# The low-rank mixer on array tiles: A summed in column tiles, V.A in row tiles, u kept by feature chunk

## The chip, the cores and the metric

One NeuronCore of a Trainium2 chip runs the program. Its engines each follow their own instruction list and wait for one another through semaphores: PE (TensorE, matrix products; its weight loads are listed as PEld), DVE (VectorE), ACT (ScalarE), POOL (GpSimd) and SP (SyncE, which here only issues DMAs). PE reads SBUF and writes PSUM, which has eight banks of 512 float32 values per partition; DVE and ACT take the products out of PSUM. The metric is the device time of one execution in microseconds. The kernel before took 309.22 us, the median of three runs (308.85 to 309.67).

## The reference

For 8 batches of 8 heads, 576 tokens and 64 features a head, a cosine-weighted linear attention gives x; a mixer over tokens of rank 32 and a two-layer network over features follow:

```
phi(t)  = [relu(t) cos(theta_s), relu(t) sin(theta_s)]       theta_s = pi/2 * s/576
kv      = phi(k)^T v,  z = sum_s phi(k)                        per batch and head
x       = phi(q) kv / (phi(q) z + 1e-6)                        [576, 512] per batch, heads side by side
A^T     = x^T U          [512, 32]                             U: [576, 32]
u       = x + (A^T V)^T                                        V: [32, 576]
out     = u + relu(u w_ch1) w_ch2                              w_ch1: [512, 2048], w_ch2: [2048, 512]
```

All inputs and the output are float32; the kernel multiplies in bfloat16 and sums in float32.

## The kernel before

The 576 tokens of a batch are four chunks of 128 (index c) and a tail of 64; the tails of two batches, an even and an odd one, share the 128 partitions of one tile, and the network runs over four such pairs of batches. The 512 features are four chunks of 128 (index d), the 2048 hidden features sixteen (index j).

The order of all work is written out by hand. The network gives `slots`: for each pair 16 turns `g1_main` of the even batch (u^T times w_ch1, four matmuls of 512 tokens' columns, then a relu on ACT), 16 of the odd one, four `g1_tail`, and 36 turns `g2_part` (hid times w_ch2, four matmuls of 512 columns; after every fourth, DVE adds u and the output tile is stored). In pair 0, sixteen turns of `g2_part` come between the two batches. A turn is about 0.86 us on PE. Everything else is hung on turns through `todo` and is issued behind that turn: the attention of the batches that come later, from `attention_plan(b)` for batches 2 to 7 (the start turn `w` from `PLAN`, offsets within it), and by hand for batch 1 (`at(...)`). Batch 0 has no network to hide behind and runs first, in `first_chain`. Engines take their instructions in the order in which they are issued here.

For one batch the steps around the change are:

- `x_unit`, `x_two`: PE multiplies phi(q) with kv for one token chunk into PSUM, DVE normalises into `x_bf` (tokens on partitions, [128, 4 chunks, 512 features]) or the tail's `x_tl`.
- `A_unit` (L416): U^T x. The rank is 32, so each token chunk c takes one of the four column tiles of the array (32 columns, `tile_position=(0, c * R)`) and leaves its own partial sum over its 128 tokens in partitions 32c to 32c+31 of one bank; the tail adds a quarter of the features into each. The cast into `A_sb` (128 x 512, bfloat16) keeps four partial sums.
- `u_unit` (L434; `u_two`, L969, for batch 1): V^T A for one token chunk is one matmul of 128 rows and 512 columns. `V_bf` holds V four times over, one copy in each 32 partitions, so that this matmul also adds the four partial sums. DVE then adds x (L448, L982) and leaves u for this token chunk in `u_bf`. The tail's matmuls (L444) do the same for two batches at once.
- `utr_dma` (L461): SP issues two DMA transposes, one for token chunks 0 and 1, one for 2 and 3, that bring u^T into `uT` for `g1_main`; a third for the tail.

Batch 0 does without the DMA: `open_mm` (L780) transposes x on PE into PSUM, `uTd_mm` (L502) adds A^T V to it there, and a cast takes the sum into `uT`; `u_dma` (L475) later transposes it back into `u_bf` for the output. Its A is made in two halves of 256 features (`a_mm`, L765 and L773).

PSUM is shared by tags: "g" (three banks) and "o" (two) belong to the network's two layers, "T" is one bank, "X" two. `spare(turn)` gives the one of "g" and "o" that the network is not using in that turn. The inputs' staging tiles `qst`, `kst`, `vst` exist once each; the loads of a later batch go out on SP when the casts have read them.

Ahead of all, `keep_warm` multiplies zeros on PE until q has come.

Of the kernel before, what the change touches and what calls it, by code (L numbers as in the profile page):

```python
# [17 lines left out]
def kernel(  # L18
# [163 lines left out]
    A_sb = [const.tile([P, DM], BF16, name=f"A_sb{i}") for i in range(4)]  # L182
# [7 lines left out]
    def keep_warm(n, tag, bufs, w=512):  # L190
        w_ps = ps.tile([P, 512], FP32, tag=tag, bufs=bufs, name="w_ps")
        for _ in range(n):
            nc.tensor.matmul(  # L193
                out=w_ps[:, 0:w], lhsT=zero[:, 0:P], rhs=zero[:, 0:w], start=True, stop=True
            )
# [220 lines left out]
    def A_unit(b, tag, bufs, eng=None, n0=0, n1=DM, a_ps=None):  # L416
        if a_ps is None:
            a_ps = ps.tile([P, DM], FP32, tag=tag, bufs=bufs, name="a_ps")
        w = (n1 - n0) // 4
        for c in range(4):  # L420
            nc.tensor.matmul(  # L421
                out=a_ps[c * R : c * R + R, n0:n1], lhsT=U_bf[:, c, :],
                rhs=x_of(b, c)[:, n0:n1], start=True, stop=False, tile_position=(0, c * R),
            )
        for c in range(4):
            ns = slice(n0 + c * w, n0 + c * w + w)
            nc.tensor.matmul(
                out=a_ps[c * R : c * R + R, ns], lhsT=U_bf[:, 4 + b % 2, :],
                rhs=x_of(b, 4)[:, ns], start=False, stop=True, tile_position=(0, c * R),
            )  # L430
        cast(eng or V_, A_of(b)[:, n0:n1], a_ps[:, n0:n1])
        return a_ps

    def u_unit(b, c, tag, bufs):  # L434
        if b not in u_bf:
            u_bf[b] = pool.tile([P, 4, DM], BF16, tag="u_bf", bufs=3, name="u_bf")
        if c == 4:
            u_tl[b // 2] = pool.tile([P, DM], BF16, tag="u_tl", bufs=2, name="u_tl")
        va = ps.tile([P, DM], FP32, tag=tag, bufs=bufs, name="va_ps")
        if c < 4:  # L440
            nc.tensor.matmul(out=va, lhsT=V_bf[:, c, :], rhs=A_of(b), start=True, stop=True)  # L441
        else:
            for i in range(2):
                nc.tensor.matmul(  # L444
                    out=va[tail(i), :], lhsT=V_tl, rhs=A_of(b - 1 + i), start=True, stop=True,
                    tile_position=(0, i * TS),
                )
        nc.vector.tensor_tensor(  # L448
            out=u_bf[b][:, c, :] if c < 4 else u_tl[b // 2], in0=x_of(b, c), in1=va,
            op=ALU.add,  # L450
        )
# [9 lines left out]
    def utr_dma(b, c0, c1):  # L461
        if c0 < 4:
            uT_alloc(b)
            nc.sync.dma_start_transpose(
                out=uT[b][:, c0:c1, :, :].rearrange("m c d t -> m (c d) t"),
                in_=u_bf[b][:, c0:c1, :].rearrange("p c n -> p (c n)"),
            )
        else:
            uTt_alloc(b // 2)
            nc.sync.dma_start_transpose(out=uT_tl[b // 2], in_=u_tl[b // 2])  # L470

    def u_dma(b, c0, c1):
        if b not in u_bf:
            u_bf[b] = pool.tile([P, 4, DM], BF16, tag="u_bf", bufs=3, name="u_bf")
        nc.sync.dma_start_transpose(  # L475
            out=u_bf[b][:, c0:c1, :].rearrange("t c (d n) -> t (c d) n", n=P),
            in_=uT[b][:, c0:c1, :, :].rearrange("n c d t -> n (c d t)"),
        )
# [18 lines left out]
    def uTd_evac(b, d, eng):  # L497
        cast(eng, uT[b][:, :, d, :], uT_ps[b, d])

    def uTd_mm(b, d):  # L500
        t = uT_ps[b, d]
        nc.tensor.matmul(  # L502
            out=t.rearrange("m c t -> m (c t)"), lhsT=A_of(b)[:, d * P : d * P + P],
            rhs=V_bf.rearrange("r c t -> r (c t)"), start=False, stop=True,
        )

    def uTt_direct(pr, tag, bufs, eng):
        uTt_alloc(pr)
        t = ps.tile([P, 4, P], FP32, tag=tag, bufs=bufs, name="uTt_ps")
        for d in range(4):  # L510
            dd = slice(d * P, d * P + P)
            nc.tensor.matmul(
                out=t[:, d, :], lhsT=x_tl[:, dd], rhs=ident, start=(d == 0), stop=False
            )
            for i in range(2):
                nc.tensor.matmul(
                    out=t[:, d, tail(i)], lhsT=A_of(2 * pr + i)[:, dd], rhs=V_tl,
                    start=False, stop=(d == 3 and i == 1),
                )
        cast(eng, uT_tl[pr], t)  # L520

# [5 lines left out]
    def g1_main(b, j, half=False):  # L527
        if b not in hid:
            hid[b] = pool.tile([P, NJ, 512], BF16, tag="hid", bufs=2, name="hid")
        g_ps = g_open.pop((b, j), None)  # L530
        d0 = 0 if g_ps is None else 2
        if g_ps is None:
            g_ps = ps.tile([P, 512], FP32, tag="g", bufs=3, name="g_ps")
        if half:
            g_open[b, j] = g_ps
        for d in range(d0, 2 if half else 4):
            nc.tensor.matmul(  # L537
                out=g_ps.rearrange("p (c t) -> p c t", c=4),
                lhsT=w1_bf[:, d, j * P : j * P + P],
                rhs=uT[b][:, :, d, :],  # L540
                start=(d == 0),
                stop=(d == 3),
            )
        if half:
            return
        nc.scalar.activation(  # L546
            out=hid[b][:, j, :], in_=g_ps, func=AF.Relu, bias=0.0, scale=1.0
        )

    def g_half(b, d, js):  # L550
        for j in js:
            if d == 0:
                g_open[b, j] = ps.tile([P, 512], FP32, tag="g", bufs=3, name="g_ps")
            nc.tensor.matmul(  # L554
                out=g_open[b, j].rearrange("p (c t) -> p c t", c=4),
                lhsT=w1_bf[:, d, j * P : j * P + P],
                rhs=uT[b][:, :, d, :],
                start=(d == 0),
                stop=False,
            )  # L560
# [23 lines left out]
    def g2_part(pr, cc, part):  # L584
# [6 lines left out]
        if cc == 4:  # L591
            b, lhs, c, u = None, hid_tl[pr], 0, u_tl[pr]
        else:
            b, c = (2 * pr, cc) if cc < 4 else (2 * pr + 1, cc - 5)
            lhs, u = hid[b], u_bf[b][:, c, :]
# [14 lines left out]
        if js[-1] < NJ - 1:  # L610
# [3 lines left out]
            out=o_sb[:, cols], in0=u[:, cols], in1=o[:, cols], op=ALU.add  # L614
# [54 lines left out]
    def attention_plan(b):  # L669
# [39 lines left out]
        for c in range(4 + odd):  # L709
            put(a_at + 2 + c, u_unit, c, tag=True)  # L710
        put(a_at + 4, utr_dma, 0, 2)
        put(a_at + 6, utr_dma, 2, 4)
        if odd:
            put(a_at + 8, utr_dma, 4, 5)
# [45 lines left out]

    def a_mm(b, a_ps, n0, n1, cs):
        w = (n1 - n0) // 4
        for c in cs:
            if c < 4:
                nc.tensor.matmul(  # L765
                    out=a_ps[c * R : c * R + R, n0:n1], lhsT=U_bf[:, c, :],
                    rhs=x_of(b, c)[:, n0:n1], start=True, stop=False,
                    tile_position=(0, c * R),
                )
                continue  # L770
            for i in range(4):
                ns = slice(n0 + i * w, n0 + i * w + w)
                nc.tensor.matmul(  # L773
                    out=a_ps[i * R : i * R + R, ns], lhsT=U_bf[:, 4 + b % 2, :],
                    rhs=x_of(b, 4)[:, ns], start=False, stop=True, tile_position=(0, i * R),
                )
# [8 lines left out]
    def first_chain(b):  # L785
# [42 lines left out]
        a_mm(b, a_ps, 0, 256, range(5))  # L828
        cast(A_, A_of(b)[:, 0:256], a_ps[:, 0:256])
# [9 lines left out]
        a_mm(b, a_ps, 256, 512, range(5))  # L839
        cast(A_, A_of(b)[:, 256:512], a_ps[:, 256:512])  # L840
# [17 lines left out]
    keep_warm(86, "X", 1, P)  # L858
# [110 lines left out]
    def u_two(b, c0):  # L969
        if b not in u_bf:  # L970
            u_bf[b] = pool.tile([P, 4, DM], BF16, tag="u_bf", bufs=3, name="u_bf")
        if c0 == 0:
            t = ps.tile([P, 2, 512], FP32, tag="X", bufs=1, name="va2_ps")
            va = [t[:, 0, :], t[:, 1, :]]
        else:
            va = [ps.tile([P, DM], FP32, tag="T", bufs=1, name="va_ps"), side["g"]]
        for c in (c0, c0 + 1):
            nc.tensor.matmul(
                out=va[c - c0], lhsT=V_bf[:, c, :], rhs=A_of(b), start=True, stop=True
            )  # L980
        for c in (c0, c0 + 1):
            nc.vector.tensor_tensor(  # L982
                out=u_bf[b][:, c, :], in0=x_of(b, c), in1=va[c - c0], op=ALU.add
            )

    at(22, lambda: A_unit(1, "T", 1, A_))
    for n, c0 in enumerate((0, 2)):
        at(23 + n, lambda c0=c0: u_two(1, c0))
        at(23 + n, lambda c0=c0: utr_dma(1, c0, c0 + 2))
    at(32, lambda: u_unit(1, 4, *O2))  # L990
# [71 lines left out]
```

## Time and profile before

| what | us |
|---|---|
| median of the runs | 309.22 |
| the profiled execution | 311.43 |
| its span, first to last instruction | 309.7 |
| PE busy in it | 301.4 |
| DVE busy | 149.7 |
| ACT busy | 140.7 |
| POOL busy | 46.5 |
| four V.A matmuls of a batch (L441), each | 0.379, starts 0.216 apart when back to back |
| the add of u for one chunk (L448), mean | 0.686 |
| the cast of A on DVE (L110, 128 x 512) | 0.692 |

A matmul's length in the trace includes its way through the array, in which the next has already begun; what a matmul costs PE is the distance from start to start. A group of lines in the timeline is written as its first start, the time from that to the last end, and the count. The granted clock is the share of TensorE's full clock that the chip gave it, 0.998 on the mean of this execution.

### The profile page before, as it was taken

Reading aid. Unit: us, or ns where it says so; the run is one execution under the profiler, and the core shown is the slowest. Engines: PE = TensorE matmul, PEld = TensorE weight load, DVE = VectorE, ACT = ScalarE, POOL = GpSimd, SP = SyncE. Lnnn points to the kernel's source line nnn. Section 1 sums busy time; section 2 is a strip of 40 time slices with the busy share of each in tenths; the row PEclk is TensorE's granted clock in tenths of the full one; section 3 lists DMA queues with packets and bytes.
Section 4 is the critical chain, followed back from the end, with each engine's and each line's share of the span. In section 5 each row is a group of like instructions: output and inputs, shape, how many; then the busy total and the mean of one; then the engine's idle time right before and its main releaser. Section 6 shows DMA issues by size and latency. Waiting matters only on the chain.

```text
span 309.7 us, 5867 instructions
## 1 busy us (share of the span) xinstructions
PE 301.4 (97%) x2392; PEld 161.0 (52%) x2392; DVE 149.7 (48%) x353; ACT 140.7 (45%) x241; POOL 46.5 (15%) x86
## 2 busy tenths in 40 slices
PE   8999999999999999999999999999999999999992
PEld 8676454448455444664454444664455444554441
DVE  4978574864867692256247590166336500001211
ACT  2945912365771566589000566589100566620000
POOL 8411200020020015004311400004221000000000
PEclk9999999999999999999999999999999999999999
DMA  7999999899999989798999399812941220002212
GB/s 209 353 260 255 247 183 226 228 220 237 290 156 225 295 186 244 220 296 180 196 276 341 99 167 243 249 19 77 222 110 70 68 51 2 0 22 82 68 68 70
DMA packets 90702, 54.28 MB, mean 175 GB/s; under 512 B 58484, under 2 KB 87444, under 8 KB 90676
## 3 DMA queue, kind: packets, MB, share of 16 engines
q1 hardware_dynamic: 84020, 43.72, 61.2%
q0 software_dynamic: 5984, 9.60, 13.0%
q10 hardware_dynamic: 672, 0.59, 0.7%
q8 instruction: 19, 0.31, 0.4%
q14 instruction: 7, 0.06, 0.1%
HBM read 36.86 MB, written 9.44 MB: 149 GB/s over the span
## 4 chain that ended last, share of the span: by engine, by line
PE 86%; DMA 6%; SPq 3%; DVE 3%; issue 1%; DVEq 0%
PE o_ps L603 38%; PE g_ps L537 31%; DMA vst<-in_v_dram 6%; PE gt_ps L569 5%; PE kv_ps L305 3%; PE x_ps L396 2%; PE va_ps L441 2%; SPq L74 1%; SPq L87 1%; PE a_ps L421 1%; PE t_ps L322 1%; DVE u_bf L982 1%; DVE v_ext L110 1%; DVE k_p L266 0%; PE g_ps L554 0%
## 5 line engine op out<-in xcount | busy, mean ns | idle before, releaser
L546 ACT ACTIVATE hid<-g_ps 128x512 bf16<-128x512 f32 x128 | 76.2, 599 | 106.2 <-PE g_ps L537 106.2
L603 PE MATMUL o_ps<-w_bf,hid 128*128 128x512 bf16 (+2 forms) x528 | 119.7, 372 | 0.0
L537 PE MATMUL g_ps<-uT,w_bf 128*128 128x512 bf16 x506 | 115.4, 379 | 0.0
L537 PEld LDWEIGHTS <-w_bf 128*128 128x128 bf16 x506 | 48.0, 98 | 56.7 <-issue 1.9
L603 PEld LDWEIGHTS <-hid 128*128 128x128 bf16 x528 | 48.5, 98 | 51.9 <-issue 1.1
L613 DVE TENSOR_TENSOR o_sb<-u_bf,o_ps 128x512 f32<-128x512 bf16 (+2 forms) x33 | 22.1, 670 | 57.0 <-PE o_ps L603 56.8
L628 POOL DMA_DIRECT2D out_dram<-o_sb x18 | 11.4, 632 | 122.2 <-DVE o_sb L613 48.1
L110 POOL CAST v_ext<-vst 128x512 bf16<-128x512 f32 (+1 forms) x26 | 18.5, 735 | 48.8 <-DMA vst<-in_v_dram 48.7
L110 DVE CAST kv<-kv_ps 128x260 bf16<-128x260 f32 (+1 forms) x15 | 6.4, 427 | 36.1 <-PE kv_ps L305 36.1
L448 DVE TENSOR_TENSOR u_bf<-x_bf,va_ps 128x512 bf16<-128x512 bf16 x24 | 16.5, 686 | 10.2 <-PE va_ps L441 10.2
L369 DVE TENSOR_SCALAR rec<-x_ps 128x8 f32<-128x8 f32 (+2 forms) x39 | 6.3, 162 | 20.1 <-PE x_ps L396 19.4
L569 PE MATMUL gt_ps<-uT_tl,w_bf 128*128 128x128 bf16 x256 | 15.9, 219 | 0.0
L406 DVE TENSOR_TENSOR x_bf<-x_ps,rec 128x512 bf16<-128x512 f32 x22 | 15.2, 692 | 0.8
L569 PEld LDWEIGHTS <-w_bf 128*128 128x128 bf16 x256 | 14.7, 98 | 0.9
L603 PE MATMUL o_ps<-w_bf,hid_tl 128*128 128x512 bf16 x64 | 14.8, 379 | 0.0
L305 PEld LDWEIGHTS <-k_p 128*128 128x128 bf16 x256 | 11.2, 97 | 3.4 <-issue 0.3
L576 ACT ACTIVATE hid_tl<-gt_ps 128x512 bf16<-128x512 f32 x16 | 9.6, 598 | 6.6 <-PE gt_ps L569 6.6
L305 PE MATMUL kv_ps<-v_ext,k_p 128*128 128x65 bf16 (+1 forms) x256 | 11.9, 193 | 0.2
L264 ACT ACTIVATE k_p<-kst,sinw 128x512 bf16<-128x512 f32 x17 | 12.0, 717 | 0.0
L266 DVE TENSOR_SCALAR q_p<-qst,cosw 128x512 bf16<-128x512 f32 x21 | 9.9, 481 | 3.2 <-DMA qst<-in_q_dram 3.2
L193 PE MATMUL w_ps<-zero 128*128 128x128 bf16 (+1 forms) x97 | 10.1, 269 | 1.2 <-DVE zero L119 1.2
L266 DVE TENSOR_SCALAR k_p<-kst,cosw 128x512 bf16<-128x512 f32 x20 | 10.4, 542 | 1.8 <-DMA kst<-in_k_dram 1.8
(143 smaller groups left out, 252.0 us busy)
## 6 DMA issues: line engine op xcount, KB each, us to landing
kst<-in_k_dram SPq DMA_DIRECT2D x14, 512.0 KB, 8.0
qst<-in_q_dram SPq DMA_DIRECT2D x13, 512.0 KB, 5.3
vst<-in_v_dram SPq DMA_DIRECT2D x12, 512.0 KB, 8.0
out_dram<-o_sb POOLq DMA_DIRECT2D x18, 256.0 KB, 3.8
w_bf<-in_moe_w_ch_dram POOLq DMA_DIRECT2D x8, 512.0 KB, 12.9
out_dram<-o_sb SPq DMA_DIRECT2D x13, 256.0 KB, 2.4
qst<-in_q_dram SPq DMA_DIRECT2D x2, 640.0 KB, 8.0
kst<-in_k_dram SPq DMA_DIRECT2D x2, 640.0 KB
```

Source lines behind the costliest of these rows:

```text
L110: eng.tensor_copy(out=o, in_=i)
L264: nc.scalar.activation(out=o, in_=i, func=AF.Relu, bias=0.0, scale=w)
L266: eng.tensor_scalar(out=o, in0=i, scalar1=0.0, scalar2=w, op0=ALU.max, op1=ALU.mult)
L305: nc.tensor.matmul(out=acc[:, i, :], lhsT=k_of(b, c, h), rhs=v_tl[:, h, 0:n] if c == 4 and b < 2 else vx[:, c, h, 0:n], start=(c == 0), st ...
L406: nc.vector.tensor_tensor(out=x_of(b, c, rows).rearrange("p (g i d) -> p g i d", g=2, d=D), in0=view[:, :, :, 0:D], in1=rec[rows].unsqueez ...
L448: nc.vector.tensor_tensor(out=u_bf[b][:, c, :] if c < 4 else u_tl[b // 2], in0=x_of(b, c), in1=va, op=ALU.add,)
L537: nc.tensor.matmul(out=g_ps.rearrange("p (c t) -> p c t", c=4), lhsT=w1_bf[:, d, j * P : j * P + P], rhs=uT[b][:, :, d, :], start=(d == 0) ...
L546: nc.scalar.activation(out=hid[b][:, j, :], in_=g_ps, func=AF.Relu, bias=0.0, scale=1.0)
L569: nc.tensor.matmul(out=g_ps[:, jj, :], lhsT=w1_bf[:, d, j * P : j * P + P], rhs=uT_tl[pr][:, d, :], start=(d == 0), stop=(d == 3),)
L603: nc.tensor.matmul(out=o[:, cols], lhsT=lhs[:, j, c * P : c * P + P], rhs=w2_bf[:, j, cols], start=(j == 0), stop=(j == NJ - 1),)
L613: nc.vector.tensor_tensor(out=o_sb[:, cols], in0=u[:, cols], in1=o[:, cols], op=ALU.add)
L628: eng.dma_start(out=out[b].rearrange("(m k) n -> m k n", k=9)[:, c : c + 6 : 5, cols], in_=o_sb[:, cols],)
```

## The change

- A: each column tile now belongs to a feature chunk j, not to a token chunk. It takes the five token chunks (the tail first) one after another in the same 128 columns of PSUM, so that the sum over tokens is whole. `A_sb` becomes 128 x 128: partitions 32j to 32j+31 hold the 32 ranks of feature chunk j. The cast is of 128 columns.
- V.A: feature chunk j is now in 32 partitions of its own, so the products for the four j are put on the four row tiles of the array (32 rows each, `tile_position=(j * R, 0)`), each into its own PSUM bank, with `c` as the outer loop: sixteen matmuls of 128 columns instead of four of 512. They take both banks of "X" and two spare ones at the same time (`four_banks`). The tail is eight such matmuls, on 32 x 64 tiles.
- u: the four adds are now by feature chunk, and `u_bf` and `uT` are laid out feature chunk first. The two transposes of a batch are of feature chunks 0 and 1, and 2 and 3, and are issued one turn earlier in the plan. The output's adds read u in four runs of 128.
- Batch 0: the halves of A are column tiles 0, 1 and 2, 3; `uTd_mm` uses one row tile of 32 rows.
- The zero products in front are 4 of 512 columns and 72 of 128, instead of 86 of 128.

```diff
-    A_sb = [const.tile([P, DM], BF16, name=f"A_sb{i}") for i in range(4)]
+    A_sb = [const.tile([P, P], BF16, name=f"A_sb{i}") for i in range(4)]
...
-    def keep_warm(n, tag, bufs, w=512):
+    def keep_warm(n, tag, bufs, short=0):
         w_ps = ps.tile([P, 512], FP32, tag=tag, bufs=bufs, name="w_ps")
-        for _ in range(n):
+        for i in range(n + short):
+            w = 512 if i < n else P
...
+    def A_mm(b, a_ps, js):
+        for c in ORD:
+            for j in js:
+                nc.tensor.matmul(
+                    out=a_ps[j * R : j * R + R, 0:P],
+                    lhsT=U_bf[:, c if c < 4 else 4 + b % 2, :],
+                    rhs=x_of(b, c)[:, j * P : j * P + P], start=(c == ORD[0]), stop=(c == ORD[-1]),
+                    tile_position=(0, j * R),
+                )
+
+    def A_unit(b, tag, bufs, eng=None):
+        a_ps = ps.tile([P, DM], FP32, tag=tag, bufs=bufs, name="a_ps")
+        A_mm(b, a_ps, range(4))
+        cast(eng or V_, A_of(b), a_ps[:, 0:P])
+
+    def four_banks(*spare):
+        t = ps.tile([P, 2, 512], FP32, tag="X", bufs=1, name="va4_ps")
+        more = [
+            x if not isinstance(x, tuple)
+            else ps.tile([P, 512], FP32, tag=x[0], bufs=x[1], name="va_ps")
+            for x in spare
+        ]
+        return [t[:, 0, :], t[:, 1, :]] + more
...
+    def u_mm(b, *spare):
...
+        va[b] = four_banks(*spare)
         for c in range(4):
...
+            for j in range(4):
+                rows = slice(j * R, j * R + R)
                 nc.tensor.matmul(
+                    out=va[b][j][:, c * P : c * P + P], lhsT=V_bf[rows, c, :],
+                    rhs=A_of(b)[rows, :], start=True, stop=True, tile_position=(j * R, 0),
                 )
...
+    def u_add(b, j):
+        ns = slice(j * P, j * P + P)
         nc.vector.tensor_tensor(
+            out=u_bf[b][:, j, :, :], in0=x_bf[b][:, :, ns],
+            in1=va[b][j].rearrange("p (c n) -> p c n", c=4), op=ALU.add,
+        )
+
+    def u_tail(pr, *spare):
+        u_tl[pr] = pool.tile([P, DM], BF16, tag="u_tl", bufs=2, name="u_tl")
+        vt = four_banks(*spare)
+        for i in range(2):
+            for j in range(4):
+                rows = slice(j * R, j * R + R)
+                nc.tensor.matmul(
+                    out=vt[j][tail(i), 0:P], lhsT=V_tl[rows, :],
+                    rhs=A_of(2 * pr + i)[rows, :], start=True, stop=True,
+                    tile_position=(j * R, i * TS),
+                )
+        for j in range(4):
+            ns = slice(j * P, j * P + P)
+            nc.vector.tensor_tensor(
+                out=u_tl[pr][:, ns], in0=x_tl[:, ns], in1=vt[j][:, 0:P], op=ALU.add
+            )
...
     def uTd_mm(b, d):
         t = uT_ps[b, d]
         nc.tensor.matmul(
-            out=t.rearrange("m c t -> m (c t)"), lhsT=A_of(b)[:, d * P : d * P + P],
-            rhs=V_bf.rearrange("r c t -> r (c t)"), start=False, stop=True,
-        )
...
+            out=t.rearrange("m c t -> m (c t)"), lhsT=A_of(b)[d * R : d * R + R, :],
+            rhs=V_bf[d * R : d * R + R].rearrange("r c t -> r (c t)"),
+            start=False, stop=True, tile_position=(d * R, 0),
+        )
...
-        for c in range(4 + odd):
-            put(a_at + 2 + c, u_unit, c, tag=True)
-        put(a_at + 4, utr_dma, 0, 2)
-        put(a_at + 6, utr_dma, 2, 4)
+        plan.append((w + a_at + 2, lambda: u_mm(b, *[spare(w + a_at + 2)] * 2)))
+        for j in range(4):
+            put(a_at + 2 + j, u_add, j)
+        put(a_at + 3, utr_dma, 0, 2)
+        put(a_at + 5, utr_dma, 2, 4)
         if odd:
+            plan.append(
+                (w + a_at + 7, lambda: u_tail(b // 2, *[spare(w + a_at + 7)] * 2))
+            )
             put(a_at + 8, utr_dma, 4, 5)
...
-        a_mm(b, a_ps, 0, 256, range(5))
-        cast(A_, A_of(b)[:, 0:256], a_ps[:, 0:256])
+        A_mm(b, a_ps, (0, 1))
+        cast(A_, A_of(b)[0:TS, :], a_ps[0:TS, 0:P])
...
-    keep_warm(86, "X", 1, P)
+    keep_warm(4, "X", 1, 72)
...
     at(22, lambda: A_unit(1, "T", 1, A_))
-    for n, c0 in enumerate((0, 2)):
-        at(23 + n, lambda c0=c0: u_two(1, c0))
-        at(23 + n, lambda c0=c0: utr_dma(1, c0, c0 + 2))
-    at(32, lambda: u_unit(1, 4, *O2))
+    at(23, lambda: u_mm(1, T1, side["g"]))
+    for j in range(4):
+        at(23, lambda j=j: u_add(1, j))
+    for c0 in (0, 2):
+        at(23, lambda c0=c0: utr_dma(1, c0, c0 + 2))
+    at(32, lambda: u_tail(0, T1, O2))
     at(33, lambda: utr_dma(1, 4, 5))
```

More of the change, by code (lines that the diff above doesn't have):

```diff
@@ L414, in A_of @@
         return A_sb[b % 4]
[L416 to L419, printed above, removed]
-        for c in range(4):
-            nc.tensor.matmul(
-                out=a_ps[c * R : c * R + R, n0:n1], lhsT=U_bf[:, c, :],
-                rhs=x_of(b, c)[:, n0:n1], start=True, stop=False, tile_position=(0, c * R),
-            )
[L425 to L429, printed above, removed]
-            )
-        cast(eng or V_, A_of(b)[:, n0:n1], a_ps[:, n0:n1])
-        return a_ps
@@ L434, in u_unit @@
[L434 to L451, printed above, removed]
+    def A_mm(b, a_ps, js):
[7 more added lines that the diff above has]
+                )
@@ new lines @@
+    va = {}
+    def u_mm(b, *spare):
+        if b not in u_bf:
+            u_bf[b] = pool.tile([P, 4, 4, P], BF16, tag="u_bf", bufs=3, name="u_bf")
+        va[b] = four_banks(*spare)
+        for c in range(4):
+            for j in range(4):
[4 more added lines that the diff above has]
+                )
@@ new lines, in u_add @@
+    def u_add(b, j):
[10 more added lines that the diff above has]
+                rows = slice(j * R, j * R + R)
+                nc.tensor.matmul(
+                    out=vt[j][tail(i), 0:P], lhsT=V_tl[rows, :],
[4 more added lines that the diff above has]
+            ns = slice(j * P, j * P + P)
+            nc.vector.tensor_tensor(
+                out=u_tl[pr][:, ns], in0=x_tl[:, ns], in1=vt[j][:, 0:P], op=ALU.add
+            )
@@ L464, in utr_dma @@
             nc.sync.dma_start_transpose(
-                out=uT[b][:, c0:c1, :, :].rearrange("m c d t -> m (c d) t"),
-                in_=u_bf[b][:, c0:c1, :].rearrange("p c n -> p (c n)"),
+                out=uT[b][:, c0:c1, :, :].rearrange("m d c t -> m (d c) t"),
+                in_=u_bf[b][:, c0:c1, :, :].rearrange("p d c n -> p (d c n)"),
             )
@@ L473, in u_dma @@
         if b not in u_bf:
-            u_bf[b] = pool.tile([P, 4, DM], BF16, tag="u_bf", bufs=3, name="u_bf")
+            u_bf[b] = pool.tile([P, 4, 4, P], BF16, tag="u_bf", bufs=3, name="u_bf")
         nc.sync.dma_start_transpose(
-            out=u_bf[b][:, c0:c1, :].rearrange("t c (d n) -> t (c d) n", n=P),
-            in_=uT[b][:, c0:c1, :, :].rearrange("n c d t -> n (c d t)"),
+            out=u_bf[b][:, c0:c1, :, :].rearrange("t d c n -> t (d c) n"),
+            in_=uT[b][:, c0:c1, :, :].rearrange("n d c t -> n (d c t)"),
         )
@@ L497, in uTd_evac @@
     def uTd_evac(b, d, eng):
-        cast(eng, uT[b][:, :, d, :], uT_ps[b, d])
+        cast(eng, uT[b][:, d, :, :], uT_ps[b, d])
     def uTd_mm(b, d):
@@ L502, in uTd_mm @@
         nc.tensor.matmul(
-            out=t.rearrange("m c t -> m (c t)"), lhsT=A_of(b)[:, d * P : d * P + P],
-            rhs=V_bf.rearrange("r c t -> r (c t)"), start=False, stop=True,
-        )
[L507 to L520, printed above, removed]
+            out=t.rearrange("m c t -> m (c t)"), lhsT=A_of(b)[d * R : d * R + R, :],
+            rhs=V_bf[d * R : d * R + R].rearrange("r c t -> r (c t)"),
+            start=False, stop=True, tile_position=(d * R, 0),
+        )
     hid, hid_tl = {}, {}
@@ L539, in g1_main @@
                 lhsT=w1_bf[:, d, j * P : j * P + P],
-                rhs=uT[b][:, :, d, :],
+                rhs=uT[b][:, d, :, :],
                 start=(d == 0),
@@ L556, in g_half @@
                 lhsT=w1_bf[:, d, j * P : j * P + P],
-                rhs=uT[b][:, :, d, :],
+                rhs=uT[b][:, d, :, :],
                 start=(d == 0),
@@ L591, in g2_part @@
         if cc == 4:
-            b, lhs, c, u = None, hid_tl[pr], 0, u_tl[pr]
+            b, lhs, c = None, hid_tl[pr], 0
+            u = u_tl[pr].rearrange("p (j n) -> p j n", n=P)
         else:
             b, c = (2 * pr, cc) if cc < 4 else (2 * pr + 1, cc - 5)
-            lhs, u = hid[b], u_bf[b][:, c, :]
+            lhs, u = hid[b], u_bf[b][:, :, c, :]
         if last:
@@ L613, in g2_part @@
         nc.vector.tensor_tensor(
-            out=o_sb[:, cols], in0=u[:, cols], in1=o[:, cols], op=ALU.add
+            out=o_sb[:, cols].rearrange("p (j n) -> p j n", n=P),
+            in0=u[:, cols.start // P : cols.stop // P, :],
+            in1=o[:, cols].rearrange("p (j n) -> p j n", n=P), op=ALU.add,
         )
@@ L759, in warm @@
         keep_warm(n, *tag)
[L761 to L776, printed above, removed]
     def open_mm(b, d, t, cs):
@@ L838, in first_chain @@
         uTd_evac(b, 1, V_)
-        a_mm(b, a_ps, 256, 512, range(5))
-        cast(A_, A_of(b)[:, 256:512], a_ps[:, 256:512])
+        A_mm(b, a_ps, (2, 3))
+        cast(A_, A_of(b)[TS:P, :], a_ps[TS:P, 0:P])
         u2 = ps.tile([P, 2, 512], FP32, tag="X", bufs=1, name="u2")
@@ L967 @@
             at((16, 17, 18, 19, 20)[n], lambda c=c: x_unit(1, c, "X", 1))
[L969 to L984, printed above, removed]
-    at(22, lambda: A_unit(1, "T", 1, A_))
-    for n, c0 in enumerate((0, 2)):
-        at(23 + n, lambda c0=c0: u_two(1, c0))
-        at(23 + n, lambda c0=c0: utr_dma(1, c0, c0 + 2))
-    at(32, lambda: u_unit(1, 4, *O2))
+    at(22, lambda: A_unit(1, "T", 1, A_))
+    at(23, lambda: u_mm(1, T1, side["g"]))
[4 more added lines that the diff above has]
+    at(32, lambda: u_tail(0, T1, O2))
     at(33, lambda: utr_dma(1, 4, 5))
```

## The prediction

> **What bounds the kernel now.** I read the page first: busy shares, slices, the chain that ended last.
>
> ```profile
> PE 301.4 (97%) x2392; PEld 161.0 (52%) x2392; DVE 149.7 (48%) x353; ACT 140.7 (45%) x241; POOL 46.5 (15%) x86
> ...
> PE 86%; DMA 6%; SPq 3%; DVE 3%; issue 1%; DVEq 0%
> PE o_ps L603 38%; PE g_ps L537 31%; DMA vst<-in_v_dram 6%; PE gt_ps L569 5%; PE kv_ps L305 3%; PE x_ps L396 2%; PE va_ps L441 2%; SPq L74 1%; SPq L87 1%; PE a_ps L421 1%; PE t_ps L322 1%; DVE u_bf L982 1%; DVE v_ext L110 1%; DVE k_p L266 0%; PE g_ps L554 0%
> ```
>
> PE is busy 97%, at a granted clock of 0.998, and it holds 86% of the chain. So what PE no longer has to stream is time saved, unless a wait takes it. Next, PE's timeline around one batch's A and V.A (columns: start, length, engine, line, tiles, count).
>
> ```profile
> 83.30 0.59 PE L603 MATMUL o_ps<-w_bf,hid 128*128 128x512 bf16 x2
> 83.82 0.40 PE L421 MATMUL a_ps<-x_bf,U_bf 128*32 128x512 bf16 x4
> 84.05 0.23 PE L427 MATMUL a_ps<-x_tl,U_bf 128*32 128x128 bf16 x4
> 84.21 1.90 PE L603 MATMUL o_ps<-w_bf,hid 128*128 128x512 bf16 x8
> 85.95 0.38 PE L441 MATMUL va_ps<-A_sb,V_bf 128*128 128x512 bf16 x1
> ```
>
> Starts count, not lengths. Eight matmuls of 512 columns fill 84.21 to 85.95, 0.216 us each. Four matmuls on the four column tiles of the array (`128*32`) take 0.23 us together: they run side by side, and the next four follow 0.01 us after a single one's 0.216. The two L603 matmuls before them end their turn at 83.30 + 2 x 0.216 = 83.73, and A begins at 83.82: 0.09 us of drain on the way into tiles. On the way out, 84.05 to 84.21 holds 128 columns (0.056 by L569, 16 in 0.89 us), 0.01 of stagger and 0.096 of drain. So A costs 84.21 - 83.73 = 0.48 us. The four V.A matmuls L441 stand alone between L603's; the next of these starts at 86.16, so each costs 0.216: 0.86 us a batch. The tail's V.A is the third cost:
>
> ```profile
> 109.22 0.59 PE L537 MATMUL g_ps<-uT,w_bf 128*128 128x512 bf16 x2
> 109.75 0.41 PE L444 MATMUL va_ps<-A_sb,V_tl 128*64 128x512 bf16 x2
> 110.09 0.82 PE L537 MATMUL g_ps<-uT,w_bf 128*128 128x512 bf16 x3
> ```
>
> From 109.65 to 110.09 it is 0.44 us, two matmuls side by side and two drains. Last, the only wait of PE after 25 us, and the chain into it:
>
> ```profile
> 59.28 9.15 DMA vst<-in_v_dram
> ...
> 70.46 0.34 DVE v_ext L110
> ```
>
> ```profile
> 70.45 0.59 PE L305 MATMUL kv_ps<-v_ext,k_p 128*128 128x65 bf16 x4
> 70.87 0.19 PE L305 MATMUL kv_ps<-v_ext,k_tl 128*128 128x65 bf16 x1
> ```
>
> Four matmuls of 65 columns, 0.03 us each, would be followed at 70.57; the next starts at 70.87. For these 0.30 us PE stands until batch 2's v has been loaded and cast. What PE saves before 70.8 us only lengthens this wait.
>
> **The change part by part.**
>
> *V.A in row tiles.* Removed per batch: four matmuls of 512 columns, 0.863 us. Added: sixteen of 128 columns, 32 rows each, in four rounds (c) over four row tiles (j). No row tiles run side by side in this trace; the bounds are the nearest rows. From below, they behave as the column tiles do: a round is 0.056 + 0.01 = 0.066 us, four are 0.264, and with the drains 0.093 and 0.096 the block is 0.45 us, 0.41 less. From above, they go one after another: 16 x 0.056 + 0.19 = 1.08 us, 0.22 more. The drains I take as those of a 32-row matmul, which the trace has:
>
> ```profile
> 14.08 0.34 PE L876 MATMUL z_ps<-v_tl,k_p 128*128 128x1 bf16 x8
> 14.35 0.41 PE L229 MATMUL v_ps<-V_nat,four 32*128 32x512 bf16 x2
> 14.70 0.35 PE L876 MATMUL z_ps<-v_tl,k_p 128*128 128x1 bf16 x8
> ```
>
> The eight one-column matmuls, 0.025 us each, end their turn at 14.26, and L229 starts at 14.35: 0.09 again; its 512 and 64 columns, 0.216 + 0.027, leave 0.10 until 14.70. I take the lower bound, 0.45, since four streams with four sets of weights at once is what the column tiles show, and each row tile here writes a bank of its own. The Trainium skill's page "TensorE: Matmul & The Clock Gate", section "Measured speedup vs the span model", gives 3.07 times for four row tiles of 32 rows and 512 columns; by it the block is an estimated 0.863 / 3.07 + 0.19 = 0.47 us and the sum below 0.1 us smaller. No run shown here has that case yet.
>
> *A in column tiles.* Removed: four matmuls of 512 and four of 128 columns. Added: five rounds of four matmuls of 128 columns. The columns per tile are the same 640. Five rounds of 0.066 and the drains are 0.52 us against 0.48: +0.04. From above, a round may be held by its four weight loads; the nearest row is the second A of batch 0, where a round of 256 columns follows in 0.12 us (21.63 to 21.75 below). Five of those make 0.79, +0.31. I take +0.04; the 128-column round is the same shape as L427.
>
> *The tail's V.A* becomes eight matmuls of 128 columns on eight tiles (32 by 64): 0.10 + 0.03 of stagger + 0.056 + 0.10 = 0.28 us against 0.44, -0.16; in a row it would be 8 x 0.056 + 0.19 = 0.64, +0.20.
>
> *Batch 0's first chain* (20 to 25 us):
>
> ```profile
> 21.09 0.61 PE L502 MATMUL uT_ps<-V_bf,A_sb 128*128 128x512 bf16 x2
> 21.63 0.31 PE L765 MATMUL a_ps<-x_bf,U_bf 128*32 128x256 bf16 x4
> 21.75 0.22 PE L773 MATMUL a_ps<-x_tl,U_bf 128*32 128x64 bf16 x4
> ```
>
> Each half of A now uses two column tiles: five rounds of 0.059 instead of 0.12 + 0.04, +0.14 twice. The casts shrink from 128x256 (384 ns on ACT) to 64x128: ACT's 598 for 512 columns and 384 for 256 give an estimated 277, -0.11 twice, on the path into L502. L502's pairs sit on two row tiles and two banks: 0.22 instead of 0.43 with two new drains, 0 to -0.2 each; but the evacuation of the first of a pair then starts with the second's, 0.2 later than now. I take +0.1 in all, between -0.2 and +0.4 (row tiles in sequence: 0.2 more). It passes on: batch 1's u, the transposes and the loads that lead to 70.8 all follow it.
>
> *Evacuations.* The A cast on DVE falls from 128x512 (692 ns) to 128x128 (an estimated 265, by the cast kv's 407 for 256 columns); the adds u_bf stay four of 686, with x_bf read in runs of 128 (the normalisation L406 writes in runs of 64 in 692). The tail's add becomes four of 128 columns (o_sb's of that shape takes 0.286): 1.1 for 0.69 us. Hidden: DVE is 48% busy and PE waits for none of it. Uncovered, it would be the banks: V.A now takes X's two and two spare banks at once, and a tail takes all four again five turns of 0.86 us later. Batch 3's fourth add comes behind two q casts on DVE and ends near 109.2, the tail starts near 110.2: 1 us of cover. If it is gone, PE stands for what is missing, three times.
>
> *Transposes.* Same two DMA transposes of eight blocks, issued one turn earlier, on SP; each now needs two adds as before. Behind them on SP are the next loads and the q transposes. For batch 1 the second transpose left at 52.59 behind the add that ended at 52.41; the new V.A's last round starts at 49.28 + 0.09 + 0.21 = 49.58, the first add 0.27 later (as A's cast at 84.33 behind 84.06), and four adds of 0.61 from start to start end at 52.4: unchanged, and with it the loads into 70.8. The transposes land 1 to 3 us ahead of L537's first use (batch 1: 55.68 against 57.1). The u_bf of batch 0, transposed back, now needs both halves for every output: landed at 49.58, first used at 54.66, hidden.
>
> *The zero products first:* 86 of 128 columns end at 7.7 us, and PE then waits for q until 8.41. At the slow clock (0.107 for 128 columns until 4.7 us) four of 512 and 72 of 128 end at 7.8: 0. If they ran past 8.41 every us would count until v's casts at 16.15, which wait for a load anyway.
>
> **The sum.** Behind 70.8 us: six V.A, 6 x -0.41 = -2.46; six A, +0.22; three tails, -0.48; in front of it -0.53 that the wait swallows (0.30 grows to 0.8), and +0.1 of the first chain. Together -2.6 us. The profiled execution took 311.43 us, a span of 309.7 and 1.7 around it, and becomes 308.8; against the median of the runs, 309.22, it is 306.6. The next wait that could bite is batch 3's v: cast until 89.63, used at 90.27, 0.6 us of slack, of which 0.37 goes. Batch 4's casts end at 120.87 for 125.64.
>
> **Rivals.** 0.3% (0.93 us) is about what a measurement of this kernel can tell from no change.
>
> Slower: the row tiles don't overlap. V.A 1.08: 6 x 0.22 = +1.31; A +0.22; tails +0.60; first chain +0.3; before 70.8 0.46, of which the present wait takes 0.30, so +0.16. Together +2.6, 311.8 us. For it: no row of the trace has two row tiles at once. Against: the column tiles. It decides where a V.A block passes 0.89 us (nothing gained) and 1.04 (slower).
>
> Little gained: pairs of load and matmul are issued at 0.025 us as in L876, whatever the tile. V.A is then 16 x 0.025 + 0.056 + 0.19 = 0.65, 6 x -0.22; A +0.04; tails 0; first chain +0.1: -1.0, 308.2 us. Against: L421's four loads and matmuls stand within 0.01 us.
>
> A's rounds wait for their weights: twenty loads where there were eight, and a round at the row's 0.12 us: 6 x 0.31 for 6 x 0.04, 308.2 us. For it: that row is no lower, since 256 columns fill it. Against: its loads are issued with the round before and needed 0.07 us later at the shortest (21.68 to 21.75), about a 128-column round. The Trainium skill's page "TensorEngine Tiling (Array Packing)", "Restrictions", has column tiles lose the fast weight load, and the page "TensorE: Matmul & The Clock Gate", "LDWEIGHTS (loading the stationary operand)", makes 32 columns 27 ns; four in a row would be an estimated 0.107 us a round, and 307.8 us. No run shown here tells.
>
> Hidden anyway: the loads follow PE so closely that the later batches wait as batch 2 does. If only the last two batches kept their gain, it would be 2 x 0.37 + 0.16: 308.4 us. Against: 4.8 us of cover at batch 4.
>
> A wait for banks at V.A or at a tail, up to 1 us at each of three odd batches: 306.6 + 3 = 309.6.
>
> **How the numbers follow.** Forecast 0.68, in itself 305.9 to 307.6 (A's rounds up to 0.09, the first chain's ends); row tiles in sequence 0.12; issue 0.04; weights 0.06; loads 0.05; banks 0.05. Faster (below 308.3): the forecast and half of issue, weights and loads, 0.75. Same: their other half and most of banks, 0.12. Slower (above 310.1): 0.13. The range reaches from 305.7 to 309.3: it leaves out the sequence and some banks.
>
> **What would show it.** V.A's sixteen starting within 0.27 us, four at a time; A about 0.52 from the last turn to the next; tails 0.28; the wait before kv_ps at 70 us grown to some 0.8; no idle PE before V.A or a tail. Wrong: rounds of 0.22 in V.A, or waits of PE for DVE's u_bf.

## The result and the profile after

The changed kernel takes 306.31 us, the median of four runs (305.84 to 307.00), against 309.40 for the kernel before beside it: a ratio of 0.9898 with a 95% interval of 0.9863 to 0.9934, some 3.1 us (1.0%) faster. The forecast was 306.6.

The page of the changed kernel, the lines that answer to those of before (busy shares, then the chain that ended last by engine and by line):

```profile
PE 295.3 (97%) x2538; PEld 159.8 (52%) x2578; DVE 147.2 (48%) x365; ACT 139.9 (46%) x241; POOL 46.9 (15%) x86
...
PE 94%; DMA 2%; issue 1%; DVE 1%; ACT 0%; ACTq 0%
PE o_ps L615 41%; PE g_ps L548 36%; PE gt_ps L580 5%; PE kv_ps L306 3%; PE x_ps L397 3%; DMA qst<-in_q_dram 2%; PE a_ps L420 1%; PE t_ps L335 1%; PE va_ps L450 1%; PE t_ps L323 1%; PE g_ps L565 0%; PE xh_ps L756 0%; PE x_ps L940 0%; PE z_ps L877 0%; PE w_ps L194 0%
```

PE is busy for the same share of a shorter span. V.A (now L450) has gone from 2% of the chain to 1%, and the load of v, 6% before, is out of it: the chain now stays on PE from 15 us until the add for the last output. Some matmuls' records are missing from this trace (L548 has 491 of 506, L615 507 of 528); a missing one shows as a step of 0.43 us between two starts, not as a wait.

PE's timeline around A, around V.A and around a tail in the changed kernel (start, length, engine, line, tiles, count):

```profile
83.73 0.24 PE L420 MATMUL a_ps<-x_tl,U_bf 128*32 128x128 bf16 x4
83.79 0.40 PE L420 MATMUL a_ps<-x_bf,U_bf 128*32 128x128 bf16 x16
84.12 1.90 PE L615 MATMUL o_ps<-w_bf,hid 128*128 128x512 bf16 x8
```

```profile
139.77 1.90 PE L615 MATMUL o_ps<-w_bf,hid 128*128 128x512 bf16 x8
141.60 0.40 PE L450 MATMUL va_ps<-A_sb,V_bf 32*128 32x128 bf16 x16
141.93 1.04 PE L615 MATMUL o_ps<-w_bf,hid 128*128 128x512 bf16 x4
```

```profile
108.73 1.03 PE L548 MATMUL g_ps<-uT,w_bf 128*128 128x512 bf16 x4
109.69 0.26 PE L468 MATMUL va_ps<-A_sb,V_tl 32*64 32x128 bf16 x8
109.88 1.04 PE L548 MATMUL g_ps<-uT,w_bf 128*128 128x512 bf16 x3
```

A still takes 0.39 us from its first start to the next 512-column matmul, as before (83.82 to 84.21). For V.A, the eight matmuls of L615 end their turn at 139.77 + 8 x 0.216 = 141.50; the sixteen start from 141.60 on, and PE is back at 141.93: 0.43 us with both drains, for four times 0.216. Within the block the starts come in bursts of four, 3 ns apart; the second burst follows the first by 0.067 us, the others by 0.056. The tail takes 109.88 - 109.59 = 0.29 us for 0.44.

Where the 3.1 us came from is read by stage. From batch 2's first kv matmul that had all its data to the last matmul, the kernel before takes 232.98 us (70.45 + 0.30 of wait to 303.73), the changed one 230.06 (70.65 to 300.71): 2.92 us less. The parts give 6 x (0.43 - 0.86) = -2.6 for V.A, +0.04 for A and 3 x -0.15 for the tails: -3.0. The rest lies ahead of 70 us, where the start of PE's work differs from execution to execution: q reached PE at 8.41 us in the profile before and at 9.69 in the one after.

### The profile page after: what moved, and what is told of

Read it like the earlier page. It is cut to its first block, busy times and chain, and to the rows that moved or that the text cites. A ratio compares the mean times of both kernels' runs of the same rounds, so it can differ in the third digit from the quotient of the medians.

```text
span 304.6 us, 6212 instructions
## 1 busy us (share of the span) xinstructions
PE 295.3 (97%) x2538; PEld 159.8 (52%) x2578; DVE 147.2 (48%) x365; ACT 139.9 (46%) x241; POOL 46.9 (15%) x86
## 4 chain that ended last, share of the span: by engine, by line
PE 94%; DMA 2%; issue 1%; DVE 1%; ACT 0%; ACTq 0%
PE o_ps L615 41%; PE g_ps L548 36%; PE gt_ps L580 5%; PE kv_ps L306 3%; PE x_ps L397 3%; DMA qst<-in_q_dram 2%; PE a_ps L420 1%; PE t_ps L335 1%; PE va_ps L450 1%; PE t_ps L323 1%; PE g_ps L565 0%; PE xh_ps L756 0%; PE x_ps L940 0%; PE z_ps L877 0%; PE w_ps L194 0%
## 5 line engine op out<-in xcount | busy, mean ns | idle before, releaser
L615 PE MATMUL o_ps<-w_bf,hid 128*128 128x512 bf16 (+2 forms) x507 | 115.7, 372 | 1.1 <-issue 0.2
L548 PE MATMUL g_ps<-uT,w_bf 128*128 128x512 bf16 x491 | 112.7, 379 | 1.0 <-issue 0.3
L548 PEld LDWEIGHTS <-w_bf 128*128 128x128 bf16 x506 | 47.9, 98 | 55.1 <-issue 0.3
L615 PEld LDWEIGHTS <-hid 128*128 128x128 bf16 x528 | 48.2, 98 | 50.8
L457 DVE TENSOR_TENSOR u_bf<-x_bf,va_ps 128x512 bf16<-128x512 bf16 x27 | 17.2, 682 | 9.2 <-PE va_ps L450 7.1
L615 PE MATMUL o_ps<-w_bf,hid_tl 128*128 128x512 bf16 x63 | 14.7, 379 | 0.1
L265 ACT ACTIVATE q_p<-qst,sinw 128x512 bf16<-128x512 f32 x14 | 9.7, 708 | 3.9 <-DMA qst<-in_q_dram 3.9
```

Of the source, the lines that this page charges most:

```text
L265: nc.scalar.activation(out=o, in_=i, func=AF.Relu, bias=0.0, scale=w)
L457: nc.vector.tensor_tensor(out=u_bf[b][:, j, :, :], in0=x_bf[b][:, :, ns], in1=va[b][j].rearrange("p (c n) -> p c n", c=4), op=ALU.add,)
L548: nc.tensor.matmul(out=g_ps.rearrange("p (c t) -> p c t", c=4), lhsT=w1_bf[:, d, j * P : j * P + P], rhs=uT[b][:, d, :, :], start=(d == 0) ...
L615: nc.tensor.matmul(out=o[:, cols], lhsT=lhs[:, j, c * P : c * P + P], rhs=w2_bf[:, j, cols], start=(j == 0), stop=(j == NJ - 1),)
```

## The experiments

Every ratio below is to the kernel before, run beside it on the same chip.

### V.A's order turned round

```diff
     def u_mm(b, *spare):
-        for c in range(4):
-            for j in range(4):
+        for j in range(4):
+            for c in range(4):
                 rows = slice(j * R, j * R + R)
```

> Only the order of V.A's sixteen matmuls is changed: all four token chunks of one row tile, then the next tile. Theory (the gain is that four row tiles stream side by side): a block is four times three steps of 0.056 us, three of 0.003, a last 0.056 and 0.19 of drains, 0.93 us for 0.43; six blocks behind 70.8 us cost 3.0 us more, batch 1's up to 0.5: 309.3 to 309.8 us, the gain is gone. Rival (the gain comes from the shorter cast, the adds by feature chunk and the earlier transposes): 306.3 us, no change.

Measured: 305.88 us, ratio 0.9905 (0.9891 to 0.9919). Nothing lost, against the theory's 3 us. PE's timeline of this kernel:

```profile
140.94 0.43 PE L450 MATMUL va_ps<-A_sb,V_bf 32*128 32x128 bf16 x16
141.31 1.90 PE L615 MATMUL o_ps<-w_bf,hid 128*128 128x512 bf16 x7
```

The block is 0.37 us from first start to the next matmul, 0.33 in the changed kernel. Its sixteen starts are 12 to 17 ns apart, but for a step of 27 behind the fourth, though four at a time in the program stand on one row tile. So either the row tiles don't matter, or PE does not keep to the program's order between tiles. The next run tells these apart.

### V.A on one row tile

```diff
             for j in range(4):
-                rows = slice(j * R, j * R + R)
                 nc.tensor.matmul(
-                    out=va[b][j][:, c * P : c * P + P], lhsT=V_bf[rows, c, :],
-                    rhs=A_of(b)[rows, :], start=True, stop=True, tile_position=(j * R, 0),
+                    out=va[b][j][:, c * P : c * P + P], lhsT=V_bf[0:R, c, :],
+                    rhs=A_of(b)[0:R, :], start=True, stop=True, tile_position=(0, 0),
                 )
```

> All sixteen V.A matmuls of a batch read rows 0 to 31 and stand on one row tile (its output is that of feature chunk 0 four times, so u is not the reference's); banks, sizes, counts and the adds stay. Theory (row tiles stream side by side, in whatever order they are issued): now they follow each other, 16 x 0.056 + 0.19 = 1.08 us for 0.43, seven times 0.65 = 4.5 us more: 310.0 to 310.6 us, slower than the kernel before. Rival (the smaller cast, the adds and the transposes by feature chunk make the gain): 306 us.

Measured: 310.52 us, ratio 1.0035 (1.0015 to 1.0056). The gain is gone and a little more, as the theory has it. The timeline of this kernel:

```profile
142.91 1.06 PE L449 MATMUL va_ps<-A_sb,V_bf 32*128 32x128 bf16 x16
143.91 1.47 PE L614 MATMUL o_ps<-w_bf,hid 128*128 128x512 bf16 x6
```

The starts are 0.056 us apart (the second 0.067 behind the first), and the block takes 1.00 us to the next matmul, 1.09 with the drain ahead of it, for 0.43. Seven such blocks are 4.6 us, and the ratios differ by 0.0137, 4.2 us. Banks, sizes, count, casts, adds and transposes are those of the changed kernel: V.A's gain is that the four row tiles stream side by side. And since two matmuls on one row tile need 0.056 us, starts 12 to 17 ns apart, as in the run before, can only be matmuls of different tiles. The fifth of them comes 0.067 us behind the first, as the second on one tile does here, so the first four are the first of each tile: PE started three of them ahead of others that the program has first.

### A's order turned round

```diff
     def A_mm(b, a_ps, js):
-        for c in ORD:
-            for j in js:
+        for j in js:
+            for c in ORD:
                 nc.tensor.matmul(
```

> Only the order of A's matmuls is changed: all five token chunks of one column tile, then the next tile. Theory (rounds over the column tiles keep A at its old cost): four times four steps of 0.056, a last 0.056 and 0.19 of drains, 1.15 us for 0.49; six times 0.66 behind 70.8 us, up to 0.66 for batch 1 and 0.17 for each half in batch 0: 310.3 to 311.3 us. Rival (PE takes matmuls of other tiles ahead by itself, or the loads of weights set the pace either way): 306.3 us.

Measured: 307.19 us, ratio 0.9946 (0.9932 to 0.9960): by the ratios 1.5 us of the gain is lost, neither 4 or more nor none. The changed kernel's own interval just touches this one, but in the profile the loss is plain: from batch 2's kv to the last matmul this run takes 1.24 us more than the changed kernel. In A the order can be seen, because the first matmul of each column tile reads x_tl and the other four x_bf:

```profile
139.27 0.23 PE L420 MATMUL a_ps<-x_tl,U_bf 128*32 128x128 bf16 x1
139.33 0.22 PE L420 MATMUL a_ps<-x_bf,U_bf 128*32 128x128 bf16 x1
139.34 0.23 PE L420 MATMUL a_ps<-x_tl,U_bf 128*32 128x128 bf16 x1
139.39 0.24 PE L420 MATMUL a_ps<-x_bf,U_bf 128*32 128x128 bf16 x2
139.41 0.23 PE L420 MATMUL a_ps<-x_tl,U_bf 128*32 128x128 bf16 x1
139.44 0.25 PE L420 MATMUL a_ps<-x_bf,U_bf 128*32 128x128 bf16 x3
139.48 0.23 PE L420 MATMUL a_ps<-x_tl,U_bf 128*32 128x128 bf16 x1
139.50 0.44 PE L420 MATMUL a_ps<-x_bf,U_bf 128*32 128x128 bf16 x10
139.87 1.47 PE L615 MATMUL o_ps<-w_bf,hid 128*128 128x512 bf16 x6
```

The second tile's first matmul, sixth in the program, starts at 139.34, when only two of the first tile's five can have started; the third tile's, eleventh, at 139.41, as the sixth to start. So PE does take matmuls of free tiles ahead, the experiment's rival. But here each new tile joins 0.07 us after the one before, and the block takes 0.60 us to the next matmul for 0.39. Six times 0.21 is 1.26 us, the loss behind batch 2's kv; with batch 1's it is 1.5. Why column tiles join more slowly than V.A's row tiles (0.013 us) was not tried.

### The zero products, and the transposes' turns

```diff
-    keep_warm(4, "X", 1, 72)
+    keep_warm(0, "X", 1, 86)
```

> The zero products in front are 86 of 128 columns again. Theory: 0, PE waits for q behind both, 306.3 us. Rival (the new mixture brings the clock up sooner or ends nearer to q): slower by up to 0.6 us.

Measured: 305.57 us, ratio 0.9897 (0.9882 to 0.9912).

```diff
-        put(a_at + 3, utr_dma, 0, 2)
-        put(a_at + 5, utr_dma, 2, 4)
+        put(a_at + 4, utr_dma, 0, 2)
+        put(a_at + 6, utr_dma, 2, 4)
```

> The two transposes of a batch go back to the turns they had before, one later each. Theory: 0, they land 1 us or more ahead of their use, 306.3 us. Rival (the earlier transposes carry part of the gain): PE waits before the first turn of the even or odd batch, up to one turn of 0.86 us in each of six batches, up to 311 us.

Measured: 305.84 us, ratio 0.9894 (0.9878 to 0.9909). Both equal the changed kernel's 0.9898, whose own interval reaches 1.1 us to either side: no part of the gain larger than that is theirs. For the transposes the profile tells more: from batch 2's kv to the last matmul this run takes 230.06 us, as the changed kernel does. The profiled execution with the old turns took 306.97 us though, where the three others took 305.45, 305.46 and 306.21, and its timeline, in a stretch where its program is that of the changed kernel, shows the wait for batch 2's v:

```profile
69.91 0.19 PE L306 MATMUL kv_ps<-v_ext,k_p 128*128 128x65 bf16 x1
70.67 0.22 PE L306 MATMUL kv_ps<-v_ext,k_p 128*128 128x65 bf16 x2 [0.57 <-POOL v_ext L110]
71.28 0.19 PE L306 MATMUL kv_ps<-v_ext,k_p 128*128 128x65 bf16 x1 [0.39 <-DVE v_ext L110]
```

Five matmuls that follow at 0.03 us elsewhere take from 69.91 to 71.31: 1.3 us of wait, which is most of the distance to the faster two.

### The kernel before, once more

> The kernel before once more, for a second profile of it. Theory: the 2.2 us by which its first profiled execution stood over the median were the last store (5.9 us from the last matmul's start to the end, 3.9 in every profile of the changed kernel), and the wait of 0.30 us for batch 2's v differs from execution to execution: this one ends 3.9 us behind its last matmul at about 309 us. Rival: the longer end belongs to the kernel before, and the change took 2 us from it: again 5.9.

Measured: 309.86 us, a span of 307.5; the time itself is 0.9 us over the expected 309. The ends of the first profile of before, then of this one (last matmul, last store's issue):

```profile
303.73 0.22 PE L603 MATMUL o_ps<-w_bf,hid 128*128 128x128 bf16 x1
...
304.31 0.62 ACTq L628 DMA_DIRECT2D out_dram<-o_sb  x1
```

```profile
303.62 0.22 PE L603 MATMUL o_ps<-w_bf,hid 128*128 128x128 bf16 x1
...
304.19 0.61 ACTq L628 DMA_DIRECT2D out_dram<-o_sb  x1
```

The last matmuls are 0.11 us apart, but the first span ended at 309.7, this one at 307.5, 3.9 us behind its last matmul, as the profile of the changed kernel does (300.71 to 304.6). In the trace, the last store's last packet ended at 307.79 us in the first profile and at 305.82 in this one. So 2.0 of the 2.2 us by which the first profiled execution stood over its median were a last store that landed late, not a property of the kernel, and the two first profiles' spans, 309.7 and 304.6, must not be set against each other: they differ by 5.1 us, the kernels by 3.1. The wait for v is absent here: the first four kv matmuls start at 70.63 and the next at 70.75. Behind it, 232.99 us to the last matmul, as in the first profile without its wait.

### Less work early, less work late

```diff
             cols, js = slice(0, DM), range(part * 4, part * 4 + 4)
+            if pr == 0 and cc < 4 and part == 1:
+                js = range(4, 6)
```

> Eight matmuls of 512 columns, 1.73 us of PE, are left out of pair 0's second layer between 44 and 57 us (the output of four token chunks lacks two of sixteen hidden chunks). Theory (the loads of batch 2 set 70 us, and a saving before them is swallowed as the prediction had it): PE waits about 1.4 us more before batch 2's kv, 305.3 to 305.6 us. Rival (the loads end early enough or follow PE): 304.1 us.

Measured: 305.47 us, ratio 0.9876 (0.9850 to 0.9902).

```diff
             cols, js = slice(0, DM), range(part * 4, part * 4 + 4)
+            if pr == 1 and cc < 4 and part == 1:
+                js = range(4, 6)
```

> The same eight matmuls' worth is left out of pair 1's second layer, behind 130 us (the output lacks the same share there). Both theories: nothing waits there, 1.73 us less, 304.1 us; the measure for the run that leaves them out early.

Measured: 304.19 us, ratio 0.9842 (0.9818 to 0.9866): 1.73 us less work late gives 0.0056 x 309.4 = 1.7 us, early 0.0022 x 309.4 = 0.7. That work saved early is worth less agrees with the prediction's idea of a swallowed saving, though the early run's own interval reaches to no gain and the two runs' intervals overlap a little. The early run also met the theory's 305.3 to 305.6 us, but by luck, because the place does not agree. In the profile of the run with less work early, the wait before batch 2's kv is 0.16 us. PE stands elsewhere, in front of batch 1's A:

```profile
47.83 0.33 PE L420 MATMUL a_ps<-x_bf,U_bf 128*32 128x128 bf16 x10
48.32 0.22 PE L420 MATMUL a_ps<-x_bf,U_bf 128*32 128x128 bf16 x1 [0.15 <-ACT x_bf L952]
48.73 0.27 PE L420 MATMUL a_ps<-x_bf,U_bf 128*32 128x128 bf16 x5 [0.19 <-ACT x_bf L952]
```

The last six of twenty wait 0.31 and 0.35 us for the normalised x of batch 1; 0.23 was lost in front of its last x and 0.2 at 57 us, and with the 0.16 these are 1.25 of the 1.73 us. The work left out was the cover of that chain on DVE and ACT. So this run does not show that the loads set 70 us; it shows that there is little left to be saved between 44 and 57 us before the attention of batch 1 becomes the bound.

## Why the prediction was right, point by point

- **V.A, -0.41 a batch.** Measured -0.43, and shown to be the concurrency of the row tiles by the run on one row tile. Behind the first, the rounds are 0.056 us apart, without the 0.01 that was added to each for the stagger: the next round's first matmul needs only its own tile. The estimate from the Trainium skill's page "TensorE: Matmul & The Clock Gate", "Measured speedup vs the span model", 0.47 us, came out 0.04 long. The drains, 0.19 into and out of the tiles together, came out as forecast. The row of L876 does not quite give the first of them: eight matmuls of 0.025 us from 14.08 end at 14.28, which leaves 0.07 until L229 at 14.35. That of A (83.73 to 83.82) does.
- **A, +0.04, up to +0.31.** Measured +0.01. The rounds of 128 columns stand 0.056 us apart, so four weight loads fit into one; the rival in which they don't is out, and with it the 0.107 us a round that was worked out from the Trainium skill's pages.
- **Tails, -0.16.** Measured -0.15.
- **First chain, +0.1, between -0.2 and +0.4.** From the first A to the first g1 turn it is 4.06 and 3.92 us in the two profiles of before and 4.14 in that of the change. In three later profiles of the same chain (old zero products, old turns, less work late) it is 4.36 to 4.78, because PE stands 0.2 to 0.6 us for the load of w_bf (start to start), which the prediction did not have. Whether the kernel before would stand there too when q comes as early is not shown.
- **Evacuations, 0.** The casts and adds of the changed kernel, by form:

```profile
L457 DVE TENSOR_TENSOR u_bf<-x_bf,va_ps 128x512 bf16<-128x512 bf16 x27 | 17.2, 682 | 9.2 <-PE va_ps L450 7.1 <-PE side L450 2.1
L475 DVE TENSOR_TENSOR u_tl<-x_tl,va_ps 128x128 bf16<-128x128 bf16 x16 | 3.5, 279 | 4.3 <-PE va_ps L468 4.3
L110 DVE CAST A_sb<-a_ps 128x128 bf16<-128x128 f32 x6 | 1.7, 292 | 3.8 <-PE a_ps L420 3.8
```

  682 ns for 686, 279 for an assumed 286, 292 for an estimated 265. PE never waits for a bank: of the changed kernel's blocks none starts later than its drain allows. Batch 3's fourth add ended at 108.6 and the tail started at 109.69.
- **Transposes and zero products, 0.** The two runs that put them back show no difference: for the transposes none behind 70 us, for the zero products none that the interval of 1.1 us could show.
- **The 0.53 us ahead of 70.8 us that the wait for v swallows.** This is the step that failed. The wait was to grow from 0.30 to 0.8 us; in the profile of the change there is none. The fifth kv matmul follows the first by 0.12 us, as four of 0.03 make it, and DVE's last cast of v ends at 70.35, 0.30 us ahead of the first:

```profile
70.65 0.29 PE L306 MATMUL kv_ps<-v_ext,k_p 128*128 128x65 bf16 x4
70.77 0.19 PE L306 MATMUL kv_ps<-v_ext,k_tl 128*128 128x65 bf16 x1
```

```profile
69.94 0.41 DVE L110 CAST v_ext<-vst 128x512 bf16<-128x512 f32 x1
```

  In the second profile of before that cast ends 0.93 us ahead; with the old turns PE waits 1.3 us. So the wait is not the kernel's but the execution's, and it swallows a saving only where v comes late. The saving itself is seen: from the first g1 turn to batch 2's first kv it is 46.11 and 45.81 us in the two profiles of before, 45.25 in that of the change, and 45.24, 45.25 and 45.39 in the three later profiles named above, 0.4 us or more below the better one of before. On one row tile it is 45.91, longer by the 0.66 of batch 1's V.A.
- **The sum, -2.6.** As measured, the parts are -2.92 behind 70.8 us, where the forecast had -2.72, -0.56 ahead of it for 0, and +0.1 to +0.2 of the first chain: about -3.3 where v and w_bf are in time. The medians give -3.1. So the forecast of 306.6 is close to 306.31 although its account of the wait is wrong: that term is small beside the six V.A blocks, which were right, and the interval of 1.1 us to either side can't tell the sums apart.
- **The rivals.** Row tiles in sequence were out from the profile, and built, V.A on one row tile took 310.5 us where the rival said 311.8, which had the tails and batch 0 in sequence too. Issue at 0.025 us a pair is out too: sixteen pairs start within 0.19 us. No wait for banks was seen, and the later batches don't wait for loads.

## What to carry to other kernels

Where a product has 32 rows or 32 columns, put what else needs that shape on the other tiles: four row tiles, each on a PSUM bank of its own (sharing one was not tried), gave 0.43 us for 0.86, drains included. Of that 0.43, 0.19 is the way into and out of tiles, so short blocks pay it for little. Issue such blocks with the tile as the innermost index: the other order cost 0.03 us a block on the row tiles and 0.21 on the column tiles. Read a wait in one profile as one execution's until a second profile has it too, and compare two spans only when you know how each of them ends.

## What the runs showed of the hardware that was not expected

PE does not start matmuls on different tiles in program order. With five in a row on one column tile, the first matmul of the second tile, sixth in the program, was the third to start, 0.07 us into the block; with four in a row on one row tile, all sixteen started 12 to 17 ns apart but for one step of 27, where two on the same tile need 0.056 us. The Trainium skill's page "TensorE: Matmul & The Clock Gate", "The mechanism", has matmuls start and end strictly in order; for the starts on different tiles these two runs say otherwise.

The first loads vary: q's first transposes on PE began between 8.33 and 9.73 us in the ten profiles of this study. In four of them the program is the same from the first A to batch 2's kv (the changed kernel, old zero products, old turns, less work late). The three early ones (8.33 to 8.58) stood 0.2 to 0.6 us for the load of w_bf near 22 us and began batch 2's kv between 69.75 and 69.91; the late one (9.69) did not stand there and began it at 70.65.
